# Loading, band, mixing and stores of a convolution plus spectral-mixing kernel: full-row loads, an on-chip band, four modes at a time, 8-tile stores

## The chip, the cores and the metric

The kernel runs on one core of one Trainium2 chip. Such a core has a matrix engine (TensorE, PE in the profile; its weight loads are listed as PEld), a vector engine (DVE), a scalar engine (ACT), GpSimd (POOL), and SyncE (SP), which here only issues DMAs. Each engine works through its own queue in order; DMAs are carried out by 16 DMA engines. The metric is the device time of one execution in microseconds (us).

## The reference

`x` is [8, 3264, 192] in float32 (batch B, sequence S, channels D). It passes first through a causal convolution of 7 taps whose softmaxed weights differ by head (8 heads of 24 channels), then through a spectral step over the sequence: the first 64 Fourier modes are multiplied by a complex 192x192 matrix for each mode, transformed back and added, and a ReLU of a channel product is added to that.

```python
# convolution: w = softmax(weight) per head, x padded with 6 zero rows at the front
out = np.einsum('hk,bskhg->bshg', w, x_unf)
# spectral step on u0 = out
X  = np.fft.rfft(x, axis=1);  Xr, Xi = real(X[:, :64]), imag(X[:, :64])
Yr = einsum('bmd,mde->bme', Xr, w_r) - einsum('bmd,mde->bme', Xi, w_i)
Yi = einsum('bmd,mde->bme', Xr, w_i) + einsum('bmd,mde->bme', Xi, w_r)
y  = np.fft.irfft(Y, n=S, axis=1)
u  = x + y
return u + np.maximum(u @ w_ch, 0.0)
```

## The kernel before

The sequence is cut into 27 windows of 122 rows; a window is loaded with the 6 rows ahead of it, so it fills 128 partitions. All of x stands in SBUF as bf16 (`x_all`), and the convolved values overwrite it in place. A batch is worked on in three units of 10, 8 and 9 windows.

1. **Load (POOL's DMA queue).** `load_mid` (L63) loads the windows of one unit, all 128 rows. Windows 0 and 26 of all eight batches come in two DMAs of their own (L71 with 122 partitions, L73 with 98), which are issued second and fourth. At most eight DMAs of this queue are outstanding; each issue waits for the one eight places before it.
2. **Band and Fourier tables (setup).** The softmax is worked out on 8 partitions, written to a DRAM scratch (`vdram`), read back as `hank` (L116) in a skewed form and reversed into `cband` (L118), a 128x128 band for each head. DVE prepares the angles, ACT the sines (`fst`, L143).
3. **Convolution stage.** For each batch: eight matmuls a unit against `cband` into two PSUM buffers (L208), ACT casts them back into `x_all` (L214); `dft` is 27 matmuls against `fst` into one PSUM buffer `xp` (L247), which DVE copies to `xs` (L250); `xtrans` transposes `xs` (L257, L259) and DVE spreads it into `xt` (L261). In between `t_part` transposes the convolved windows (L225: 128 channels at a time; L222: the last 64 channels of two windows, side by side on two column halves), and DVE copies them into `cT` (L241).
4. **Mixing stage.** It needs `xt` of all batches. For two modes at a time (a group `wt`, two DMAs of 144 KB, five buffers) the weights are the stationary operand and `xt` (16 columns) moves: 12 matmuls a group (L306). Every 8 modes DVE and ACT copy the result into `yeT` (L316, L318). The rest of the transposes is interleaved here.
5. **Output stage.** 54 groups, each of two windows of two batches: PE forms `zp` (inverse transform and channel product, L355 to L360) and `yp` (L361); ACT takes the ReLU (L366, three buffers `r`), DVE adds `x_all` (L374) into `t` (three buffers), POOL or, every third time, DVE adds `r` (L377), SP stores `t` with four DMAs (L385), of 112 and of 10 rows for each batch.

The order on each engine is set by the framework's scheduler, from the program's order and its dependencies; waits are semaphores.

Of the kernel before, what the change touches and what calls it, by code (L numbers as in the profile page):

```python
# [18 lines left out]
def kernel(  # L19
# [33 lines left out]
    dramp = ctx.enter_context(tc.tile_pool(name="dscr", bufs=1, space=bass.MemoryType.DRAM))  # L53
# [35 lines left out]
    xt = ep.tile([P, 3, MODES, 2 * B], BF16, tag="xt")  # L89

    vdram = dramp.tile([H, 256], BF16, name="vdram")
    with tc.tile_pool(name="setup", bufs=1) as sp:
        wrev = sp.tile([H, KK], F32, tag="wrev")
        nc.sync.dma_start(out=wrev[:], in_=bass.AP(tensor=weight.tensor, offset=weight.offset,
                                                   ap=[[KK, H], [1, KK]]))
        vrow = sp.tile([H, 256], BF16, tag="vrow")
        nc.vector.memset(vrow[:], 0.0)
        nmax = sp.tile([H, 1], F32, tag="nmax")
        nc.vector.reduce_max(out=nmax[:], in_=wrev[:], axis=AX.X)
        wsub = sp.tile([H, KK], F32, tag="wsub")  # L100
        nc.vector.tensor_scalar(out=wsub[:], in0=wrev[:], scalar1=nmax[:, 0:1], scalar2=None,
                                op0=ALU.subtract)
        wexp = sp.tile([H, KK], F32, tag="wexp")
        nc.scalar.activation(out=wexp[:], in_=wsub[:], func=ACT.Exp)
        wsum = sp.tile([H, 1], F32, tag="wsum")
        nc.vector.reduce_sum(out=wsum[:], in_=wexp[:], axis=AX.X)
        nc.vector.tensor_scalar(out=wsum[:], in0=wsum[:], scalar1=1e-9, scalar2=None, op0=ALU.add)
        wrec = sp.tile([H, 1], F32, tag="wrec")
        nc.vector.reciprocal(out=wrec[:], in_=wsum[:])

        nc.vector.tensor_scalar(out=vrow[:, 127:127 + KK], in0=wexp[:], scalar1=wrec[:, 0:1],
                                scalar2=None, op0=ALU.mult)
        nc.sync.dma_start(out=vdram[:], in_=vrow[:])
        va = vdram[:]
        hank = sp.tile([P, H, P], BF16, tag="hank")
        nc.sync.dma_start(out=hank[:], in_=bass.AP(tensor=va.tensor, offset=va.offset,  # L116
                                                   ap=[[1, P], [256, H], [1, P]]))
        nc.vector.tensor_copy(out=cband[:], in_=hank[:, :, ::-1])  # L118
# [6 lines left out]
                       allow_small_or_imprecise_dtypes=True)  # L125
        kprod = sp.tile([P, NWIN, MODES], F32, tag="kprod")
        nc.vector.tensor_tensor(out=kprod[:],
# [3 lines left out]
        for comp in range(2):  # L131
            targ = sp.tile([P, NWIN, MODES], F32, tag=f"targ{comp}")
            shift = float(S // 4) if comp == 0 else 0.0
            nc.vector.tensor_scalar(out=targ[:], in0=kprod[:], scalar1=shift, scalar2=1.0 / S,  # L134
                                    op0=ALU.add, op1=ALU.mult)
            nc.vector.tensor_scalar(out=targ[:], in0=targ[:], scalar1=MAGIC, scalar2=None, op0=ALU.add)
            nc.vector.tensor_scalar(out=targ[:], in0=targ[:], scalar1=-MAGIC, scalar2=-float(S),
                                    op0=ALU.add, op1=ALU.mult)
            nc.vector.scalar_tensor_tensor(out=targ[:], in0=targ[:], scalar=shift, in1=kprod[:],
                                           op0=ALU.add, op1=ALU.add)  # L140
            nc.vector.tensor_scalar(out=targ[:], in0=targ[:], scalar1=-float(S) / 2,
                                    scalar2=float(S) / 2, op0=ALU.max, op1=ALU.min)
            nc.scalar.activation(out=fst[:, :, MODES * comp:MODES * comp + MODES], in_=targ[:],  # L143
                                 func=ACT.Sin, scale=(TWOPI / S) * (1.0 if comp == 0 else -1.0))


    for b in range(1, B):
        load_mid(b, 1, 9)
        load_mid(b, 10, 8)
        load_mid(b, 18, 8)  # L150
# [28 lines left out]
    yeT = [constp.tile([P, B, 2 * MODES], BF16, tag=f"yeT{t}", name=f"yeT{t}") for t in range(2)]  # L179
    zwi = constp.tile([P, 2, B, D], BF16, tag="zwi")  # L180
# [6 lines left out]
    wp = early_stack.enter_context(tc.tile_pool(name="wts", bufs=5, side="right"))  # L187
# [7 lines left out]

    ps1 = ExitStack()
# [19 lines left out]
    def t_slot(o, b, slot):  # L216
        i, r = divmod(slot, 3)
        w = min(2 * i, NWIN - 2) if r == 2 or (i == PAIRS and r == 1) else 2 * i + r
        idw = ident[0:WIN, 0:WIN]
        if r == 2 or (i == PAIRS and r == 1):  # L220
            for k in range(2):
                nc.tensor.transpose(o[64 * k:64 * k + 64, :], x_all[0:WIN, b, w + k, P:D], idw,  # L222
                                    tile_position=(0, 64 * k))
        else:
            nc.tensor.transpose(o, x_all[0:WIN, b, w, 0:P], idw)  # L225
# [6 lines left out]
    def t_unit_halves(b, u):  # L232
        s0, n = USLOTS[u]
        h1 = (n + 1) // 2
        return [(b, s0, h1), (b, s0 + h1, n - h1)]

    def t_part(b, s0, n):
        tp = ptr.tile([P, 8 * WIN], BF16, tag="tp")
        for k in range(n):
            t_slot(tp[:, WIN * k:WIN * k + WIN], b, s0 + k)  # L240
        nc.vector.tensor_copy(out=cT[:, b, WIN * s0:WIN * (s0 + n)], in_=tp[:, 0:WIN * n])  # L241
# [11 lines left out]
    def xtrans(b, xs):  # L253
        tp = pxx.tile([P, 3, P], F32, tag="xt")
        xsv = xs[:, :].rearrange("k (p j) -> k j p", j=3)
        for j in range(3):
# [5 lines left out]
            out=xt[:, :, :, b:2 * B:B].rearrange("p j m c -> p j c m"),  # L262
# [3 lines left out]
    tq = []  # L266
    pend = None
    for b in range(B):
        for u in range(3):
            conv_unit(b, u)  # L270
            if u == 0 and b > 0:
                pend = (b - 1, dft(b - 1))
            if u == 1 and pend is not None:
                xtrans(*pend)
                pend = None
            if b < 5:
                for _ in range(2):
# [147 lines left out]
```

## Time and profile before

| | us |
|---|---|
| median of 3 runs (lowest, highest) | 309.76 (309.28, 312.28) |
| the profiled execution: its time | 309.76 |
| the profiled execution: its span | 308.0 |
| busy in the span: PE, DVE, POOL, ACT | 201.0, 142.8, 136.9, 99.8 |

The span is the time between the first and the last event that the profile shows; 1.76 us lie outside of it. No engine is busy for more than two thirds of the span, so the shares say little; the stages have to be read one by one. A matmul's end is modelled, so a busy PE is not PE at its peak. [...]

### The profile page before, as it was taken

The page shows a single profiled execution, that of the slowest core. Times are in us where ns is not written, and L with a number is a line of the kernel's source. Part 1 is how long each engine was busy: PE and PEld are TensorE (multiplying, and loading weights), DVE is VectorE, ACT ScalarE, POOL GpSimd, SP SyncE. Part 2 cuts the span into 40 slices and gives each one's busy share as a digit, 9 for nine tenths or more (in the row PEclk, how much of TensorE's full clock was granted, in tenths as well). Part 3 has the DMA queues.
Part 4 walks back from the last instruction along what each step waited for, and adds up shares of the span by engine and source line. Part 5 has one row for each costly group of instructions (what it writes and reads, how often), then busy time and mean ns, then how long its engine had stood idle before and what let it go on. Part 6 is the DMA issues. An engine that isn't in the chain of part 4 may idle for free.

```text
span 308.0 us, 5139 instructions
## 1 busy us (share of the span) xinstructions
PE 201.0 (65%) x1971; PEld 144.0 (47%) x1971; DVE 142.8 (46%) x174; ACT 99.8 (32%) x123; POOL 136.9 (44%) x145
## 2 busy tenths in 40 slices
PE   0004865999999989996232598776775666665610
PEld 0003543776778966554232376545553544544500
DVE  6009902386454444443000155565566456556560
ACT  1003696001468822001000145333433434334320
POOL 8804644625000046336763044546546444564650
PEclk9999997899999975555555589799799999999975
DMA  8899999997500049657999026656565556656653
GB/s 93 49 180 191 191 191 192 192 145 100 91 2 3 0 56 166 95 81 111 176 202 157 0 63 180 177 135 178 151 183 159 142 153 168 178 159 168 180 162 85
DMA packets 74160, 40.73 MB, mean 132 GB/s; under 512 B 39824, under 2 KB 74136, under 8 KB 74136
## 3 DMA queue, kind: packets, MB, share of 16 engines
q0 software_dynamic: 44240, 20.08, 50.5%
q1 hardware_dynamic: 29896, 20.33, 24.7%
q8 instruction: 15, 0.25, 0.3%
q14 instruction: 9, 0.07, 0.1%
HBM read 40.35 MB, written 20.06 MB: 196 GB/s over the span
## 4 chain that ended last, share of the span: by engine, by line
PE 35%; DMA 24%; POOL 12%; DVE 8%; ACT 7%; issue 6%; SPq 6%; DVEq 0%; POOLq 0%; ACTq 0%
DMA out_dram<-t 11%; POOL t L377 10%; PE tp L225 8%; DMA x_all<-in_x_dram 8%; PE tp L222 7%; PE xp L247 7%; DVE t L374 6%; SPq L385 6%; PE cp L208 5%; DMA wt<-in_moe_w_i_dram 5%; ACT x_all L214 4%; PE yps L306 2%; POOL wt L192 2%; ACT r L366 1%; PE tp L289 1%
## 5 line engine op out<-in xcount | busy, mean ns | idle before, releaser
L377 POOL TENSOR_TENSOR t<-t,r 122x768 f32<-122x768 f32 x36 | 64.8, 1806 | 70.0 <-DVE t L374 41.6
L374 DVE TENSOR_TENSOR t<-yp,x_all 122x768 f32<-122x768 f32 (+1 forms) x54 | 51.4, 956 | 49.7 <-DMA out_dram<-t 33.5
L366 ACT ACTIVATE r<-zp 122x768 f32<-122x768 f32 (+1 forms) x54 | 43.7, 810 | 70.8 <-POOL t L377 54.7
L214 ACT CAST x_all<-cp 122x960 bf16<-122x960 f32 (+2 forms) x48 | 39.0, 886 | 59.9 <-PE cp L208 59.8
L355 PE MATMUL zp<-zwi,gst 128*128 128x384 bf16 x108 | 36.7, 340 | 32.0 <-ACT r L366 28.6
L359 PE MATMUL zp<-win,cT 128*128 128x192 bf16 x216 | 48.7, 255 | 0.0
L208 PE MATMUL cp<-x_all,cband 128*128 128x240 bf16 (+2 forms) x192 | 26.7, 276 | 30.3 <-DMA x_all<-in_x_dram 26.7
L241 DVE COPY cT<-tp 128x854 bf16<-128x854 bf16 (+2 forms) x48 | 28.8, 606 | 38.1 <-PE tp L222 17.8
L192 POOL DMA_DIRECT2D wt<-in_moe_w_r_dram x32 | 19.3, 602 | 57.7 <-PE yps L306 47.3
L359 PEld LDWEIGHTS <-cT 128*128 128x128 bf16 x216 | 21.8, 101 | 42.7 <-issue 39.6
L64 POOL DMA_DIRECT2D x_all<-in_x_dram x24 | 25.2, 1057 | 27.5 <-DMA x_all<-in_x_dram 26.5
L225 PE MATMUL tp<-ident,x_all 122*128 122x122 bf16 x216 | 36.5, 255 | 0.0
L208 PEld LDWEIGHTS <-cband 128*128 128x128 bf16 x192 | 18.5, 104 | 35.2 <-DVE targ L134 26.7
L361 PE MATMUL yp<-zwi,gst 128*128 128x384 bf16 x108 | 28.9, 343 | 4.3 <-DVE t L374 4.3
L222 PE MATMUL tp<-ident,x_all 122*64 122x122 bf16 x224 | 31.6, 274 | 0.0
L306 PE MATMUL yps<-xt,wt 128*128 128x16 bf16 x384 | 14.9, 175 | 20.8 <-DMA wt<-in_moe_w_i_dram 14.6
L247 PE MATMUL xp<-x_all,fst 122*128 122x192 bf16 (+1 forms) x216 | 24.7, 260 | 3.9 <-ACT fst L143 3.9
L360 PEld LDWEIGHTS <-cT 128*128 128x128 bf16 x216 | 21.8, 101 | 9.9 <-issue 1.7
L360 PE MATMUL zp<-win,cT 128*128 128x192 bf16 x112 | 26.2, 257 | 0.0
L306 PEld LDWEIGHTS <-wt 128*128 128x128 bf16 x384 | 13.6, 105 | 22.6 <-issue 9.2
L360 PE MATMUL zp<-wB,cT 128*128 128x192 bf16 x104 | 22.5, 255 | 0.0
L192 POOL DMA_DIRECT2D wt<-in_moe_w_i_dram x32 | 19.6, 612 | 5.1 <-DMA x_all<-in_x_dram 2.9
(69 smaller groups left out, 185.6 us busy)
## 6 DMA issues: line engine op xcount, KB each, us to landing
out_dram<-t SPq DMA_DIRECT2D x104, 168.0 KB
x_all<-in_x_dram POOLq DMA_DIRECT2D x16, 384.0 KB, 16.7
wt<-in_moe_w_r_dram POOLq DMA_DIRECT2D x32, 144.0 KB, 4.8
wt<-in_moe_w_i_dram POOLq DMA_DIRECT2D x32, 144.0 KB, 5.1
x_all<-in_x_dram POOLq DMA_DIRECT2D x8, 432.0 KB, 16.9
out_dram<-t SPq DMA_DIRECT2D x104, 15.0 KB
out_dram<-t SPq DMA_DIRECT2D x2, 276.0 KB
x_all<-in_x_dram POOLq DMA_DIRECT2D x1, 366.0 KB, 23.3
```

The source lines that it names most:

```text
L192: nc.gpsimd.dma_start(out=wt[64 * half:64 * half + 64, :, :, :], in_=src[MG * g:MG * g + MG, :, :].rearrange("m (p j) e -> p m j e", j=3))
L208: nc.tensor.matmul(cp[:, j, 0:GRP * n].rearrange("p (w e) -> p w e", w=n), cband[:, h, :], x_all[:, b, w0:w0 + n, GRP * h:GRP * h + GRP], ...
L214: nc.scalar.copy(out=dst, in_=srcv)
L222: nc.tensor.transpose(o[64 * k:64 * k + 64, :], x_all[0:WIN, b, w + k, P:D], idw, tile_position=(0, 64 * k))
L225: nc.tensor.transpose(o, x_all[0:WIN, b, w, 0:P], idw)
L247: nc.tensor.matmul(xp[:, 0:D], fst[0:k, c, :], x_all[0:k, b, c, :], start=(c == 0), stop=(c == NWIN - 1))
L355: nc.tensor.matmul(zp[:, k, 0:2 * D], glhs, zwi[:, 0, 2 * q:2 * q + 2, :], start=True, stop=False)
L359: nc.tensor.matmul(o, cT[:, b, WIN * sa:WIN * sa + P], win0[:, 0:D], start=False, stop=False)
L360: nc.tensor.matmul(o, cT[:, b, WIN * sb:WIN * sb + P], wBs[par], start=False, stop=(i == 1))
L366: nc.scalar.activation(out=r[0:n, :, :], in_=zp[0:n, :, 0:2 * D], func=ACT.Relu)
L374: nc.vector.tensor_tensor(out=tv, in0=yv, in1=xv, op=ALU.add)
L377: eng.tensor_tensor(out=t[0:n, :, :], in0=t[0:n, :, :], in1=r[0:n, :, :], op=ALU.add)
```

## The change

- Loads go unit by unit in the order of use (`load_unit`), each of 128 partitions; windows 0 and 26 are now loaded with their unit. Only the first and the last window of all are loaded in two pieces (112 and 10 rows, 96 and 2 rows). For batches 1 to 7, window 0 is loaded with the 6 rows of the batch before, and DVE then overwrites those rows with zeros (L77).
- `cband` is built on the chip: the taps are broadcast to 128 partitions, POOL makes seven diagonal masks, and DVE adds them up with 56 instructions of 128x128. The angle tables take one chain of five DVE instructions, not two, and ACT makes the cosine from the absolute value.
- `dft` of a batch is written two batches later, not one; the transposes are nearly all left to the mixing stage. The last 64 channels of a unit are first copied together by DVE (`make_tail`), so that two windows are transposed by one matmul of 128 channels.
- Mixing: four modes at a time, each on its own 32 columns of the array. `xt` (of a mode and its neighbour, 32 columns) is now stationary and the weights (192 columns) move. ACT copies the product to `ymix`, two transposes bring it into the layout of before. Six `wt` buffers, not five.
- A `t` buffer holds two groups (8 tiles of 122x192), and is stored by four DMAs of twice the size. Still three buffers of `t` and of `r`.

```diff
+    def load_unit(b, u):
+        w0, n = UNITS[u]
+        if b == 0 and u == 0:
+            nc.gpsimd.dma_start(out=x_all[OV:OV + 112, 0, 0, :], in_=x[0, 0:112, :])
+            nc.gpsimd.dma_start(out=x_all[OV + 112:P, 0, 0, :], in_=x[0, 112:WIN, :])
+            load_win(0, 1, n - 1)
...
+        else:
+            load_win(b, w0, n)
+        if u == 0 and b > 0:
+            nc.vector.memset(x_all[0:OV, b, 0, :], 0.0)
...
-        nc.sync.dma_start(out=hank[:], in_=bass.AP(tensor=va.tensor, offset=va.offset,
-                                                   ap=[[1, P], [256, H], [1, P]]))
-        nc.vector.tensor_copy(out=cband[:], in_=hank[:, :, ::-1])
+        for h in range(H):
+            nc.vector.tensor_scalar(out=cband[:, h, :], in0=maskk[:, 0, :], scalar1=wsb[:, h, 0:1],
+                                    scalar2=None, op0=ALU.mult)
+            for k in range(1, KK):
+                nc.vector.scalar_tensor_tensor(out=cband[:, h, :], in0=maskk[:, k, :],
+                                               scalar=wsb[:, h, k:k + 1], in1=cband[:, h, :],
+                                               op0=ALU.mult, op1=ALU.add)
...
-    tq = []
+    tq = [(b, u) for b in range(B) for u in range(3)]
     pend = None
-    for b in range(B):
+    for b in range(B + 2):
         for u in range(3):
-            conv_unit(b, u)
-            if u == 0 and b > 0:
-                pend = (b - 1, dft(b - 1))
+            if b < B:
+                conv_unit(b, u)
+            if u == 0 and b >= 2:
+                pend = (b - 2, dft(b - 2))
...
-                for j in range(3):
-                    nc.tensor.matmul(o, wt[:, mj, j, 64 * t:64 * t + P], xt[:, j, m, :],
-                                     start=(j == 0), stop=(j == 2))
...
+    for g in range(MODES // 4):
+        yp = pconv.tile([P, 512], F32, tag="cv", name="yp")
+        for j in range(3):
+            for pos in range(4):
+                m = 4 * g + pos
+                wt = wtiles[m // MG]
+                nc.tensor.matmul(yp[32 * pos:32 * pos + 32, 0:D],
+                                 xt[:, j, m:m + 2, :].rearrange("p m k -> p (m k)"),
+                                 wt[:, m % MG, j, :], start=(j == 0), stop=(j == 2),
+                                 tile_position=(0, 32 * pos))
+        ymix = workp.tile([P, D], BF16, tag="ymix")
+        nc.scalar.copy(out=ymix[:], in_=yp[:, 0:D])
+        if tq:
+            t_unit(*tq.pop(0))
...
-            for i in range(2):
-                dst = out[2 * q0 + i, WIN * w0:WIN * (w0 + 2), :].rearrange("(k p) e -> p k e", k=2)
-                for r0, r1 in ((0, 112), (112, WIN)):
-                    nc.sync.dma_start(out=dst[r0:r1], in_=t[r0:r1, :, D * i:D * i + D])
...
+            t = p3.tile([P, 4, 2 * D], F32, tag="t")
+            npair = min(2, PAIRS - i0)
+            for i in range(i0, i0 + npair):
+                group([(q, 2 * i), (q, 2 * i + 1)], t, 2 * (i - i0))
+            store(q, 2 * i0, 2 * npair, t)
```

Two places show how the engines' queues change. The first is DVE's queue between the angle tables and the first copy of `xp` to `xs`. Before, the tables are followed by copies of transposes (`cT`) and then by `xs`:

```order
L139 SCALAR_TENSOR_TENSOR targ<-targ,kprod 128x1728 [waits DVE_49] x2
L141 TENSOR_SCALAR targ<-targ 128x1728 [waits DVE_49] x2
L183 MEMSET cT 128x8x3 [waits DMAHW1_49,Activation_49]
L241 COPY cT<-tp 128x976 [waits PE_49]
L241 COPY cT<-tp 128x854 [waits PE_49]
L241 COPY cT<-tp 128x732 [waits PE_49] x2
L250 CAST xs<-xp 128x192 [waits PE_49]
```

In the changed kernel the seven memsets of L77 stand among the tables and ahead of the first `xs` (L275); each waits on one of the eight semaphores of POOL's DMA queue (DMASW), that of its batch's first unit. Ahead of this piece stand those of batches 1 to 4; the three in it are those of batches 5, 6 and 7 (`tl` is the tail of a unit):

```order
L152 TENSOR_SCALAR kprod<-kprod 128x1728 [waits DVE_49]
L233 COPY tl<-x_all 122x640 [waits DMASW2_49,DMASW1_49,Activation_49]
L233 COPY tl<-x_all 122x512 [waits Activation_49]
L77 MEMSET x_all 6x96 [waits DMASW1_49]
L235 COPY tl<-x_all 122x512 [waits DVE_49,DMASW4_49,PE_49,Activation_49]
L236 COPY tl<-x_all 122x128
L77 MEMSET x_all 6x96 [waits DMASW4_49]
L194 MEMSET cT 128x8x3 [waits Activation_49]
L266 COPY cT<-tp 128x976
L266 COPY cT<-tp 128x854
L77 MEMSET x_all 6x96 [waits DMASW7_49]
L275 CAST xs<-xp 128x192 [waits PE_49]
```

So the first `xs` has moved behind the landing of the first unit of the last batch.

The second place is PE's queue where the first `xs` is transposed. In the changed kernel it comes right behind the 66th of the 192 convolution matmuls (before: behind the 80th, and nothing ahead of its `xs` on DVE waits for a load):

```order
L220 LDWEIGHTS cband [waits DMASW2_49]
L220 MATMUL cp<-x_all,cband 128x216 [waits Activation_49]
L220 LDWEIGHTS cband
L220 MATMUL cp<-x_all,cband 128x216
L282 LDWEIGHTS xs [waits DVE_49]
L282 MATMUL tp<-ident,xs 64x128
L284 LDWEIGHTS xs
L284 MATMUL tp<-perm,xs 64x128 [waits Pool_49]
```

Everything behind these rows on PE, 126 convolution matmuls among them, has moved behind that copy on DVE.

## Rows read from the trace of the kernel before

**Rows 1.** Windows by stage: us, busy time (instructions) by engine, PEclk, DMA share, GB/s.

```profile
0.00:26.70 26.70, 0.00 (x0) 0.00 (x0) 9.02 (x17) 1.49 (x2) 13.00 (x18) 1.00 1.13 118
...
50.00:110.50 60.50, 59.51 (x630) 45.74 (x631) 32.48 (x46) 25.21 (x31) 13.27 (x25) 0.94 0.63 80
110.50:140.00 29.50, 29.43 (x328) 17.44 (x327) 12.05 (x22) 3.85 (x5) 13.08 (x22) 0.52 0.76 111
140.00:172.00 32.00, 10.51 (x254) 8.82 (x251) 5.17 (x8) 4.27 (x6) 18.93 (x32) 0.50 0.94 149
172.00:300.50 128.50, 85.83 (x664) 61.71 (x663) 72.39 (x76) 45.86 (x58) 64.81 (x36) 0.93 0.56 152
```

**Rows 2.** Windows, two stretches of the loads.

```profile
8.00:16.00 8.00, 0.00 (x0) 0.00 (x0) 0.00 (x0) 0.00 (x0) 6.03 (x10) 1.00 0.85 50
...
22.00:64.00 42.00, 29.76 (x224) 20.12 (x225) 22.09 (x25) 20.75 (x23) 20.96 (x27) 0.92 1.60 192
```

**Rows 3.** Timeline of the opening: start, us, engine, line, operation [idle before].

```profile
3.31 3.51 POOL L71 DMA_DIRECT2D x_all<-in_x_dram  x1
...
26.75 1.76 PE L208 MATMUL cp<-x_all,cband 128*128 128x240 bf16 x8 [26.75 <-DMA x_all<-in_x_dram]
...
74.16 0.59 POOL L192 DMA_DIRECT2D wt<-in_moe_w_r_dram  x1 [1.45 <-DMA x_all<-in_x_dram]
```

**Rows 4.** Timeline of ACT late in the convolution stage, six casts a row.

```profile
93.56 4.80 ACT L214 CAST x_all<-cp 122x768 bf16<-122x768 f32 x6 [1.16 <-PE cp L208]
98.70 4.80 ACT L214 CAST x_all<-cp 122x768 bf16<-122x768 f32 x6 [0.34 <-PE cp L208]
```

**Rows 5.** Waits, the line of the weight loads: us in total, times, longest.

```profile
POOL wt L192 <- PE yps L306: 47.3, 11, 33.6
```

**Rows 6.** Timeline of PE early in the mixing stage: start, us, operation, count.

```profile
112.67 0.97 PE L289 MATMUL tp<-ident,fst 122*128 122x122 bf16 x8
...
113.86 0.31 PE L222 MATMUL tp<-ident,x_all 122*64 122x122 bf16 x2
```

**Rows 7.** Groups of instructions by form: busy us, mean ns | idle before.

```profile
L377 POOL TENSOR_TENSOR t<-t,r 122x768 f32<-122x768 f32 x36 | 64.8, 1806 | 70.0 <-DVE t L374 41.6 <-DMA out_dram<-t 21.9 <-ACT r L366 6.1
L374 DVE TENSOR_TENSOR t<-yp,x_all 122x768 f32<-122x768 f32 x52 | 49.5, 956 | 49.1 <-DMA out_dram<-t 32.9 <-PE yp L361 11.4 <-PE zp L360 2.8
...
L377 DVE TENSOR_TENSOR t<-t,r 122x768 f32<-122x768 f32 x16 | 17.3, 1081 | 1.6
...
L241 DVE COPY cT<-tp 128x854 bf16<-128x854 bf16 x24 | 14.6, 608 | 12.0 <-PE tp L222 7.2 <-PE tp L225 4.8
...
L139 DVE SCALAR_TENSOR_TENSOR targ<-targ,kprod 128x1728 f32<-128x1728 f32 x2 | 3.8, 1942 | 0.0
```

**Rows 8.** The chain that ended last, in the output stage: start, us, what.

```profile
240.71 0.16 PE zp L355
...
241.20 0.16 PE zp L355
...
242.29 0.97 DVE t L374
...
245.58 2.26 DMA out_dram<-t
247.88 0.96 DVE t L374
```

**Rows 9.** The same chain, around the ends of mixing and of the output stage.

```profile
110.57 0.75 PE yps L306 x24
...
171.06 0.72 ACT yeT L318
...
172.40 0.32 PE zwps L337
...
177.51 0.97 DVE t L374
...
299.42 1.04 DVE t L377
```

More of the change, by code (lines that the diff above doesn't have):

```diff
@@ L178 @@
     gst = constp.tile([P, GW], BF16, tag="gst")
-    yeT = [constp.tile([P, B, 2 * MODES], BF16, tag=f"yeT{t}", name=f"yeT{t}") for t in range(2)]
-    zwi = constp.tile([P, 2, B, D], BF16, tag="zwi")
+    yeT = constp.tile([P, 2, B, 2 * MODES], BF16, tag="yeT")
     stashp = ctx.enter_context(tc.tile_pool(name="stash", bufs=1))
@@ L194 @@
         wtiles.append(wt)
+    nc.vector.memset(xt[:, :, MODES, :], 0.0)
     ps1 = ExitStack()
@@ L214, in conv_unit, with make_tail, slot_lhsT @@
             nc.scalar.copy(out=dst, in_=srcv)
-    def t_slot(o, b, slot):
-        i, r = divmod(slot, 3)
[L218 to L223, printed above, removed]
-        else:
-            nc.tensor.transpose(o, x_all[0:WIN, b, w, 0:P], idw)
+    def make_tail(b, u):
+        w0, n = UNITS[u]
+        tl = workp.tile([P, 10, D - P], BF16, tag="tail")
+        if u < 2:
+            nc.vector.tensor_copy(out=tl[0:WIN, 0:n, :], in_=x_all[0:WIN, b, w0:w0 + n, P:D])
+        else:
+            nc.vector.tensor_copy(out=tl[0:WIN, 0:n - 1, :], in_=x_all[0:WIN, b, w0:w0 + n - 1, P:D])
+            nc.vector.tensor_copy(out=tl[0:WIN, n - 1:n + 1, :], in_=x_all[0:WIN, b, w0 + n - 2:w0 + n, P:D])
+        return tl
+    def slot_lhsT(b, u, tl, slot):
+        i, r = divmod(slot, 3)
+        w0 = UNITS[u][0]
+        if i == PAIRS:
+            if r == 0:
+                return x_all[0:WIN, b, NWIN - 1, 0:P]
+            j = NWIN - 1 - w0
+        elif r < 2:
+            return x_all[0:WIN, b, 2 * i + r, 0:P]
+        else:
+            j = 2 * i - w0
+        return tl[0:WIN, j:j + 2, :].rearrange("p w e -> p (w e)")
     def slot_of(w):
@@ new lines @@
+    for g in range(MODES // 4):
[12 more added lines that the diff above has]
+            t_unit(*tq.pop(0))
+        if gq:
+            g_part(gq.pop(0))
+        if g % 2 == 0:
+            et = pxx.tile([P, 2, 2, P], BF16, tag="xt", name="et")
+        for t in range(2):
+            nc.tensor.transpose(et[:, t, g % 2, :], ymix[:, 64 * t:64 * t + P], ident[:])
+        if g % 2 == 1:
+            m0 = 4 * (g - 1)
+            for t in range(2):
+                dst = yeT[:, t, :, :].rearrange("p b (c m) -> p b c m", c=2)[
+                    :, :, :, m0:m0 + 8].rearrange("p b c m -> p m c b")
+                srcv = et[:, t, :, :].rearrange("p g (q k) -> p (g q) k", q=4)[:, :, 0:16].rearrange(
+                    "p m (c b) -> p m c b", c=2)
@@ L335, in zwi_pair @@
             b = 2 * q + i
-            nc.tensor.matmul(zp[:, i, 0:2 * D], yeT[0][:, b, :], win0[:], start=True, stop=False)
-            nc.tensor.matmul(zp[:, i, 0:2 * D], yeT[1][:, b, :], win1[:], start=False, stop=True)
+            nc.tensor.matmul(zp[:, i, 0:2 * D], yeT[:, 0, b, :], win0[:], start=True, stop=False)
+            nc.tensor.matmul(zp[:, i, 0:2 * D], yeT[:, 1, b, :], win1[:], start=False, stop=True)
         for i in range(2):
@@ L347, with group @@
     npool = [0]
-    def group(combos):
+    def group(combos, t, k0):
         zp = pz.tile([P, 2, 512], F32, tag="z")
```

183 lines of the change are left out of this document (81 added, 102 removed).

## The prediction

> **What bounds the kernel now.** I read the windows by stage first [rows 1]. The reader is to see five stages with five limits. Until 26.7 us PE does nothing. From 50 to 110.5 PE is busy for 59.5 of 60.5 us and sets the pace. From 110.5 to 140 it is full again, but at a granted clock of 0.52. From 140 to 172 it has 10.5 us of work in 32, and the DMAs run at 149 GB/s: the weights are awaited. From 172 to 300.5 no engine is full (PE 86, DVE 72, POOL 65 of 128.5 us) and the DMAs are at a share of 0.56.
>
> The opening is explained by the loads. In their steady state they move 192 GB/s, but from 8 to 16 us only 50 [rows 2]. What was issued just before is the 122-partition load of the windows 0 (L71 at 3.31); the first convolution matmul waits for a load until 26.75, and a weight load at 74.16 still waits for a load of x [rows 3]. Convolution and `dft` together, once the data are there, need 5.14 us a batch: ACT's six casts begin at 93.56 and again at 98.70 [rows 4]. The weights stop for 33.6 us in one piece because five groups are loaded and PE has not begun to mix [rows 5].
>
> The output stage is a ring. The chain goes from DVE's add at 242.29 through POOL's add and the store, which lands at 247.84, to the DVE add at 247.88, which needed that `t` buffer [rows 8]; L374 idled 32.9 us behind stores [rows 7]. From 177.51 to 300.46 [rows 9] is 123 us for 54 groups: 2.28 us a group, 6.8 a turn of three buffers.
>
> **The change, part by part.** The sum is made against the profiled execution, whose time, 309.76, is also the median; its span is 308.0, so 1.76 us lie outside.
>
> *Loads.* A window is 128x192 values of bf16, 49 KB; 216 windows at 192 GB/s [rows 2] take 55 us. The badly spread loads are gone. I let the flow begin at 4 us and charge 2 us for a gap (POOL makes the identity and seven masks between the second unit's load and the third's) and 2 us for a landing (a store lands in 2.26 [rows 8]): x is complete at about 63, where before the queue was still held at 74.16 [rows 3]. The weights follow; 12 DMAs of 147 KB at 192 GB/s are 9 us, done by 73, before anybody needs them.
>
> *Band.* 56 DVE instructions of 128x128. The nearest row is the same operation on 1728 elements, 1.94 us [rows 7]. By its elements alone 128 of them are 0.144 us, 8 us for 56; with 0.15 of fixed cost each it is 16.5. I take 14, from about 9 us (POOL has to make the masks behind four DMA issues) to 23. The angle chain follows with some 8 us. All this is hidden under the next item, for any price up to 25 us.
>
> *The memsets of L77.* This is where I expect the loss. They stand in DVE's queue, which is in order, and each waits for a load. The last angle instruction (L152) stands behind the memset of batch 4, whose first unit is complete with window 118: 118 x 0.256 = 30 us, so about 38. Behind the one for batch 7 (199 windows, 51 us, so about 59) stands the first copy of `xp` to `xs`. PE, also in order, needs that `xs` behind 66 of its 192 convolution matmuls, and then stands still; so does ACT, which casts what PE makes. Before, nothing in these queues waited for more than the batch at hand. PE reaches that point at about 47 (tables at 38, two sines and an absolute value on ACT about 5 us, a `dft` of 4 us at the low clock). The pause is thus about 12 us, and from 59 on 126 matmuls, 5.25 batches, remain: 5.25 x 5.14 [rows 4] = 27 us. PE restarts cold, as at 50, and the mean clock of 0.94 over the 60.5 us behind that [rows 1] means 7 us at the low level; I charge 3. The last `dft` and a half and two rounds of `xs` and `xt` cost about one more period and a DVE round trip, 7 us. Mixing starts at 59 + 27 + 3 + 7 = **96 to 97**, not at 110.6 [rows 9].
>
> That it is still earlier is due to what left this stage: 266 of the 440 transposes stood ahead of the first mixing matmul on PE, now 27 of 328 do.
>
> *Mixing.* Three limits lie close together. DMA: 52 transfers of 147 KB are still to come, 7.67 MB: 40 us at 192 GB/s [rows 2], 51 at the 149 of the stage before [rows 1]. DVE: 43 copies of 0.61 us [rows 7] are 26; 21 tails lie between 0.1 us (0.144 us for 128 elements, [rows 7], is the nearest row for one input) and a copy's 0.61 each, I take 0.35, 7 us; eight `yeT` copies 6 (ACT's twin took 0.72 [rows 9]); with gaps 43. PE: about 301 transposes of 128 channels, the two-window tails now in one. At the low clock eight such took 0.97 us with the end of the last [rows 6], so at most 0.12 each, 36 us (the pair of half-width ones, 0.31 in the same rows, is gone). The 192 mixing matmuls move 192 columns each; at the low clock 384 columns take 0.32 us [rows 9], so 0.16 each: 31 us if they follow one another, 8 if four run side by side. I take 8, since the 32 columns of a mode are its own, and with the 51 other transposes 6: 50 us at the low clock, some 27 at the high one. Of 40, 43 and 50 at worst I take **47 us**, against 61 before (110.57 to 171.78 [rows 9]): the end is at **144**. `ymix` and its transposes lie on ACT, 4.3 us busy of 32 before [rows 1], and cost nothing unless the last pair is late (1 us, within the 47).
>
> What PE's clock does here decides little in my sum. From 110.5 to 140 it stood at 0.52 while PE was full of transposes and 16-column matmuls, and from 50 to 110.5 at 0.94 with transposes between `dft` and convolution [rows 1]. [...]
>
> *Output.* The way from the last `yeT` to the first DVE add stays at 5.7 us (171.78 to 177.51 [rows 9]). A ring now holds six groups. To the 6.8 us of a turn come, for a buffer whose both adds are POOL's, 1.81 for the second add [rows 7], and for all buffers about 1.4 for the doubled store (375 KB at 271 GB/s, the rate at which a share of 0.56 with 152 GB/s [rows 1] would reach 1), and up to 0.96 for the second DVE add: 9 to 10 us for six groups, 1.6 a group, 85 us. Close behind stand DVE, 54 x 0.956 + 18 x 1.08 + 2.5 = 74; the DMAs, 20 MB at 271 GB/s = 74; PE, two windows a group of 0.66 us (0.49 from `zp` to `zp` and 0.16 for `yp` [rows 8]) = 71; POOL 65. Four queues that are 75 to 85% full hold one another up; I take 1.7 a group, **92 us**, within 78 (DVE plus 5%) and 123 (nothing gained). SP issues half as many DMAs; it held none up that I can price.
>
> Sum: 144 + 5.7 + 92 = 242; from the last add to the end 7.5 (300.46 to 308.0), 249; outside the span 1.8: **251 us**.
>
> **The rivals.** *A: the pause does not bite*, because the waits of L77 are met earlier than I reckon, or the first `xs` is not needed so soon. Then loads and ACT set the pace: mixing starts at about 79, the rest as above: 233. Against it speaks that both queues are fixed; for it, that the landing times are my estimate.
>
> *B: the output stage gains nothing*, since DVE, PE and DMA hold one another up so that 2.28 us a group remain: 251 + 31 = 282. For it: DVE and POOL adds alternate in one order, and a late one stops both. Against: L374 waited for stores for 33 of its 49 idle us [rows 7].
>
> *C: the four matmuls of a row of modes do not overlap.* At the low clock 12 of them are then 1.9 us [rows 9], PE needs 73 us for the mixing, the end is 26 us later: 277. Against it: in the trace the half-width transposes run in pairs in 0.31 us for two [rows 6], about as long as one with its tail. [...] No run here shows 32-column tiles.
>
> [...]
>
> **How the numbers follow.** Forecast 0.78, A 0.09, B 0.06, C 0.05, D 0.02. The predicted time is the forecast's, 251. Its own bounds are the output stage's 78 to 110 and the mixing's 41 to 55: 231 to 275 when not all go one way. That leaves out B, C, D and some of the forecast's tails, and takes in A: 231 to 275. Within 1% is about what a measurement of this kernel cannot tell from no change. All cases but D are faster by more than that: faster 0.97, same 0.01, slower 0.02.
>
> **What would show it.** Right: DVE idle on a load until 55 to 62 ahead of the first `xs`, with PE and ACT idle from about 47; no stretch of 50 GB/s in the loads; the first mixing matmul at 92 to 101; weights at 150 to 195 GB/s through the mixing; stores at a share of 0.7 to 0.85. Wrong: the first `xs` before 45 (then A); a PE that is full from 97 to 170 at 0.50 (C); L401 still idle behind stores for over half of its time, or a span of over 115 us from the first to the last add (B). The weakest term is the 92 us: nothing in the trace of before shows the output stage with a longer ring.

## The result and the profile after

The changed kernel takes 263.28 us (median of 4 runs, 261.74 to 265.93) against 309.86 (309.28 to 312.28) for the kernel before: a ratio of 0.847, 95% interval 0.840 to 0.853. The prediction was 251.0 us within 231 to 275. The execution that was profiled is the longest of the four, 265.93 us with a span of 264.2 (as are those of experiments 2, 259.27, of 3 with three buffers, 288.68, and of 7 with the mixing of before, 264.09); its rows are read against its own time.

The stages first, as windows of the changed kernel (columns as in [rows 1]; PEclk is the granted clock of TensorE as a share of its full one):

```profile
8.00:16.00 8.00, 1.28 (x4) 0.41 (x4) 8.00 (x32) 0.96 (x1) 6.69 (x9) 1.00 1.48 173
12.00:60.00 48.00, 17.86 (x106) 12.77 (x106) 17.79 (x53) 19.56 (x20) 21.34 (x30) 0.74 1.60 192
...
30.20:40.00 9.80, 0.00 (x0) 0.00 (x0) 2.91 (x4) 1.21 (x1) 3.79 (x5) 0.58 1.60 192
51.00:60.80 9.80, 0.55 (x7) 0.38 (x8) 1.58 (x6) 0.00 (x0) 4.37 (x13) 0.56 1.60 191
61.00:97.50 36.50, 35.36 (x385) 31.69 (x383) 17.11 (x17) 27.91 (x34) 6.40 (x11) 0.93 0.37 54
97.50:136.00 38.50, 31.25 (x462) 23.00 (x463) 31.47 (x77) 8.18 (x18) 25.38 (x44) 0.96 1.03 155
136.00:150.50 14.50, 5.62 (x75) 2.44 (x74) 3.29 (x6) 3.56 (x8) 4.92 (x9) 0.67 0.78 122
156.20:257.00 100.80, 76.61 (x648) 57.34 (x646) 76.04 (x75) 44.31 (x57) 69.16 (x36) 0.97 0.71 194
```

The 50 GB/s of [rows 2] are gone: from 12 to 60 us the loads run at 192 without a break. In two stretches of almost 10 us PE has almost no work although the data flow. From 61 on it is full, at 0.93 of its clock. Mixing has two parts: to 136 PE and DVE are both busy for 31 of 38.5 us, then nobody is. In the output stage the DMAs moved 194 GB/s, where [rows 1] had 152.

What made the two pauses stands in the timeline of DVE, and in the waits from 20 to 66 us (us in total, times, longest us):

```profile
25.21 0.14 DVE L77 MEMSET x_all<- 6x96 uint32 x1 [1.81 <-DMA x_all<-in_x_dram]
32.16 0.14 DVE L77 MEMSET x_all<- 6x96 uint32 x1 [5.90 <-DMA x_all<-in_x_dram]
39.04 0.14 DVE L77 MEMSET x_all<- 6x96 uint32 x1 [4.93 <-DMA x_all<-in_x_dram]
39.11 0.98 DVE L152 TENSOR_SCALAR kprod<-kprod 128x1728 f32<-128x1728 f32 x1
40.02 0.50 DVE L233 COPY tl<-x_all 122x640 bf16<-122x640 bf16 x2
...
52.88 0.14 DVE L77 MEMSET x_all<- 6x96 uint32 x1 [6.39 <-DMA x_all<-in_x_dram]
...
59.85 0.14 DVE L77 MEMSET x_all<- 6x96 uint32 x1 [5.73 <-DMA x_all<-in_x_dram]
59.91 0.28 DVE L275 CAST xs<-xp 128x192 bf16<-128x192 f32 x1
```

```profile
DVE x_all L77 <- DMA x_all<-in_x_dram: 30.2, 6, 6.4
...
PE tp L264 <- DVE tl L233: 10.4, 1, 10.4
...
PE tp L282 <- DVE xs L275: 10.1, 1, 10.1
```

Each of the short zeroings but the first waits for a load, 30.2 us in all. PE's first pause ends with the tail copy at 40.02, which the transposes need; its second with the `xs` at 59.91.

The output stage by groups of instructions, 157 to 258 us:

```profile
L404 POOL TENSOR_TENSOR t<-t,r 122x768 f32<-122x768 f32 x36 | 69.2, 1944 | 43.2 <-DVE t L401 32.4 <-DMA out_dram<-t 7.9 <-ACT r L392 2.7
L401 DVE TENSOR_TENSOR t<-yp,x_all 122x768 f32<-122x768 f32 x52 | 48.1, 951 | 17.9 <-PE yp L388 14.6 <-DMA out_dram<-t 1.6 <-POOL t L404 1.1
...
L392 ACT ACTIVATE r<-zp 122x768 f32<-122x768 f32 x51 | 40.8, 809 | 45.5 <-POOL t L404 32.7 <-PE zp L387 9.1 <-PE yp L388 2.4
...
L404 DVE TENSOR_TENSOR t<-t,r 122x768 f32<-122x768 f32 x16 | 23.8, 1490 | 3.1 <-ACT r L392 2.6
```

Against [rows 7] two things moved. DVE's first add hardly waits for stores any more (1.6 us of 17.9 here, 32.9 of 49.1 before). And the second adds became longer: 1490 ns on DVE (1081 before), 1944 on POOL (1806 before), while the first add stayed at 951. By shortest, median and longest, the instructions of the second add's line:

```profile
L404 POOL TENSOR_TENSOR t<-t,r x36: 1797/1811/2545, 157.4 to 252.3; 122x768 f32<-122x768 f32 x36
...
L404 DVE TENSOR_TENSOR t<-t,r x18: 947/1358/2298, 161.6 to 256.0; 122x768 f32<-122x768 f32 x16, 92x768 f32<-92x768 f32 x2
```

And the chain of waits from 198 us on:

```profile
198.52 1.83 DVE t L401 x2
200.38 0.10 POOL t L404
200.56 2.49 POOL t L404
203.08 0.81 ACT r L392
203.94 0.32 PE zp L382
204.26 0.08 PE zp L386
```

POOL's add, which overlaps a second add of DVE begun at 200.25, takes 2.49 us in place of its shortest 1.80, and ACT's ReLU and PE's next group wait for it.

### The profile page after: what moved, and what is told of

It reads as the page before. It is cut to its first block, busy times and chain, and to the rows that moved or that the text cites. A ratio compares the mean times of both kernels' runs of the same rounds, so it can differ in the third digit from the quotient of the medians.

```text
span 264.2 us, 4507 instructions
## 1 busy us (share of the span) xinstructions
PE 172.3 (65%) x1699; PEld 130.4 (49%) x1699; DVE 154.7 (59%) x264; ACT 105.9 (40%) x140; POOL 138.7 (52%) x154
## 4 chain that ended last, share of the span: by engine, by line
PE 36%; DMA 27%; DVE 14%; POOL 12%; ACT 4%; issue 3%; SPq 1%; DVEq 0%; POOLq 0%; ACTq 0%
DMA x_all<-in_x_dram 18%; POOL t L404 7%; PE xp L272 7%; DVE t L401 6%; PE cp L220 5%; PE tp L264 5%; DMA wt<-in_moe_w_i_dram 5%; PE zp L382 4%; DMA out_dram<-t 4%; PE zp L386 4%; PE zp L387 4%; DVE cT L266 3%; PE yp L388 3%; ACT r L392 3%; PE yp L321 2%
## 5 line engine op out<-in xcount | busy, mean ns | idle before, releaser
L404 POOL TENSOR_TENSOR t<-t,r 122x768 f32<-122x768 f32 x36 | 69.2, 1944 | 43.2 <-DVE t L401 32.4
L386 PE MATMUL zp<-win,cT 128*128 128x192 bf16 x216 | 46.0, 250 | 0.0
L220 PE MATMUL cp<-x_all,cband 128*128 128x240 bf16 (+2 forms) x192 | 31.0, 297 | 20.4 <-DVE cband L128 16.4
L203 POOL DMA_DIRECT2D wt<-in_moe_w_r_dram x32 | 19.5, 611 | 44.2 <-PE yp L321 36.7
L386 PEld LDWEIGHTS <-cT 128*128 128x128 bf16 x216 | 21.4, 99 | 25.6 <-issue 23.8
L220 PEld LDWEIGHTS <-cband 128*128 128x128 bf16 x192 | 20.3, 111 | 26.3 <-DVE cband L128 17.6
L264 PE MATMUL tp<-ident,tl 122*128 122x122 bf16 x112 | 22.1, 228 | 11.1 <-DVE tl L233 10.9
L264 PE MATMUL tp<-ident,x_all 122*128 122x122 bf16 x216 | 26.4, 228 | 3.4 <-DVE cT L266 2.6
L404 DVE TENSOR_TENSOR t<-t,r 122x768 f32<-122x768 f32 (+1 forms) x18 | 25.7, 1430 | 3.3 <-ACT r L392 2.6
L388 PE MATMUL yp<-zwi,gst 128*128 128x384 bf16 x108 | 26.3, 331 | 1.2 <-DVE t L401 1.2
L387 PEld LDWEIGHTS <-cT 128*128 128x128 bf16 x216 | 21.4, 99 | 8.3 <-issue 0.7
L387 PE MATMUL zp<-win,cT 128*128 128x192 bf16 x112 | 24.0, 249 | 0.0
L264 PEld LDWEIGHTS <-x_all 122*128 122x128 bf16 x216 | 18.4, 103 | 7.2 <-issue 5.5
L272 PEld LDWEIGHTS <-fst 122*128 122x128 bf16 (+1 forms) x216 | 20.3, 106 | 2.3 <-ACT fst L156 1.2
## 6 DMA issues: line engine op xcount, KB each, us to landing
x_all<-in_x_dram POOLq DMA_DIRECT2D x9, 384.0 KB, 17.9
```

The lines of the kernel that those rows point to most:

```text
L220: nc.tensor.matmul(cp[:, j, 0:GRP * n].rearrange("p (w e) -> p w e", w=n), cband[:, h, :], x_all[:, b, w0:w0 + n, GRP * h:GRP * h + GRP], ...
L264: nc.tensor.transpose(tp[:, WIN * k:WIN * k + WIN], slot_lhsT(b, u, tl, a + k), ident[0:WIN, 0:WIN])
L272: nc.tensor.matmul(xp[:, 0:D], fst[0:k, c, :], x_all[0:k, b, c, :], start=(c == 0), stop=(c == NWIN - 1))
L386: nc.tensor.matmul(o, cT[:, b, WIN * sa:WIN * sa + P], win0[:, 0:D], start=False, stop=False)
L387: nc.tensor.matmul(o, cT[:, b, WIN * sb:WIN * sb + P], wBs[par], start=False, stop=(i == 1))
L388: nc.tensor.matmul(yp[:, k, 0:2 * D], glhs, zwi[:, 1, 2 * q:2 * q + 2, :], start=True, stop=True)
```

## The experiments

Each is an edit of the changed kernel. Stage times are from the profiled execution: first mixing matmul, end of the last `yeT`, first and last add of the output stage (97.57, 150.50, 156.22 and 256.98 us in the changed kernel). Experiment 1, in which the order on DVE came out as in the changed kernel, has 95.47, 146.56, 152.28 and 253.81 in an execution of 262.75 us; so 2 us between two profiles are no finding by themselves.

**1. The zeroings later in the program.**

```diff
-        if u == 0 and b > 0:                 # in load_unit
-            nc.vector.memset(x_all[0:OV, b, 0, :], 0.0)
             if b < B:
+                if u == 0 and b > 0:
+                    nc.vector.memset(x_all[0:OV, b, 0, :], 0.0)
                 conv_unit(b, u)
```

> Each zeroing of six rows of window 0 (L77) is moved in DVE's order from the place where the load is issued to the place where that batch's convolution is issued; nothing else changes. Theory (the zeroings hold the angle chain and the first xs behind loads, and PE and ACT behind these): first xs at 38 to 46 instead of 59.9, PE not idle for more than 5 us between 25 and 60, first mixing matmul at 72 to 80 instead of 97.6, time 238 to 246. Rival (loads of x, ACT's casts or the cold clock set the same pace once the wait is gone): first mixing matmul after 90, time 256 to 264.

263.03 us; first mixing matmul at 95.47. This did not test the theory, since DVE's order came out as before: the scheduler had put the zeroings back to where they were.

```profile
51.91 0.14 DVE L295 MEMSET x_all<- 6x96 uint32 x1 [6.40 <-DMA x_all<-in_x_dram]
...
58.86 0.14 DVE L295 MEMSET x_all<- 6x96 uint32 x1 [5.71 <-DMA x_all<-in_x_dram]
58.93 0.28 DVE L273 CAST xs<-xp 128x192 bf16<-128x192 f32 x1
```

**2. Window 0 loaded without the foreign rows**, so that no zeroing has to wait.

```diff
+        elif u == 0:
+            nc.gpsimd.dma_start(out=x_all[OV:OV + 112, b, 0, :], in_=x[b, 0:112, :])
+            nc.gpsimd.dma_start(out=x_all[OV + 112:P, b, 0, :], in_=x[b, 112:WIN, :])
+            load_win(b, 1, n - 1)
         else:
             load_win(b, w0, n)
-        if u == 0 and b > 0:
-            nc.vector.memset(x_all[0:OV, b, 0, :], 0.0)
-    nc.vector.memset(x_all[0:32, 0, 0, :], 0.0)
+    nc.vector.memset(x_all[0:32, :, 0, :], 0.0)
```

> Window 0 of every batch is loaded from row 6 on, in two DMAs of 112 and 10 rows, as batch 0 was, with the six rows zeroed once at the start: DVE has no zeroing that waits for a load. 14 more load DMAs. Theory (those waits made the two pauses of PE, 30 to 40 and 51 to 60 us): first xs at 38 to 46, first mixing matmul at 74 to 82 instead of 97.6, time 240 to 250. Rival 1 (the small loads of 10 rows slow the queue as the 122-row load did in the kernel before): loads of x end after 70 and the first mixing matmul is at 90 or later, time over 256. Rival 2 (mixing starts earlier but waits for weights that come no earlier): first mixing matmul at 74 to 82, last yeT still after 140, time 254 to 262.

254.79 us (254.18 to 259.27), 3% less. The first `dft` begins at 37.28 (44.85 in experiment 1) and the first `xs` comes at 41.82, as the theory had it, but the first mixing matmul only at 89.88: not the theory's 74 to 82, and not for rival 1's reason, since the loads did not slow (191 GB/s from 40 to 56 us). Another wait took the second pause over. The longest wait of PE, and two windows:

```profile
PE tp L286 <- POOL perm L170: 9.2, 1, 9.2
```

```profile
40.00:48.00 8.00, 7.77 (x72) 7.03 (x70) 0.71 (x2) 5.05 (x7) 4.02 (x5) 0.82 1.60 191
48.00:56.00 8.00, 0.00 (x0) 0.00 (x0) 0.00 (x0) 0.64 (x1) 4.29 (x6) 0.82 1.60 191
```

`perm`, the matrix of the second half of `xtrans`, is made by POOL behind all its issues of loads of x, and these wait for earlier loads to land (the last 16 in the changed kernel for 21.4 us together, each for 0.28 to 1.96). It is done at 56.93 here. In the changed kernel the last row of it is

```profile
51.65 0.25 POOL L168 TENSOR_SCALAR_AFFINE_SELECT perm<-perm 128x64 bf16<-128x64 bf16 x1
```

so there it was done at 51.90, 1.8 us after the second pause began (50.14), and hidden under the wait for `xs`. The other 5 us come with this experiment, which puts 14 more load DMAs ahead of `perm`.

**3. One group to a `t` buffer again; and six such buffers.**

```diff
-            t = p3.tile([P, 4, 2 * D], F32, tag="t")
             for i in range(i0, i0 + npair):
-                group([(q, 2 * i), (q, 2 * i + 1)], t, 2 * (i - i0))
-            store(q, 2 * i0, 2 * npair, t)
+                t = pt.tile([P, 2, 2 * D], F32, tag="t")   # pt: 3 buffers, or 6
+                group([(q, 2 * i), (q, 2 * i + 1)], t, 0)
+                store(q, 2 * i, 2, t)
```

> The stores alone are undone: a t buffer holds one group again, three buffers, four store DMAs per group. Theory (the ring of t set the output stage before, and six groups in it are what was gained): output back to about 2.28 us a group, 123 us in place of 101, time 282 to 288. Rival (the output stage is carried by the adds of DVE and POOL and by the ring of r, whatever the stores): time within 2% of 263.

> As the kernel with the stores undone (one group to a buffer, four store DMAs per group), but with six buffers: as many groups in the ring as in the changed kernel, in stores of half the size. Theory (the number of groups in the ring counts): time within 1% of 263. Rival (the larger stores count, by fewer issues on SP or fuller transfers): time 272 to 286.

285.48 us with three buffers: the output stage takes 125.5 us (154.25 to 279.74), and the wait of before is back:

```profile
L402 DVE TENSOR_TENSOR t<-yp,x_all 122x768 f32<-122x768 f32 x52 | 49.5, 956 | 49.0 <-DMA out_dram<-t 32.6 <-PE yp L389 10.3 <-PE zp L388 3.8
```

With six it is 264.33 us (261.63 to 264.81), and the stage 98.9 (152.60 to 251.50). So the number of groups in the ring brought the 22 us; the size of a store brought nothing that shows. DVE's second adds are the longest of all here, and the stage is none the longer for it:

```profile
L405 DVE TENSOR_TENSOR t<-t,r 122x768 f32<-122x768 f32 x16 | 30.0, 1876 | 2.0 <-ACT r L393 0.5
```

**4. Six buffers of `r`** (in bf16, so that they fit).

```diff
-        r = p3.tile([P, 2, 2 * D], F32, tag="r")
+        r = pr.tile([P, 2, 2 * D], BF16, tag="r")    # pr: 6 buffers
```

> r gets six buffers in place of three; to fit, it is kept in bf16 (the second add then reads bf16). Theory (the round of 10.4 us for six groups runs through r: a late add of POOL frees r late, ACT's next relu waits, and with it zp and PE): output 84 to 90 us instead of 101, ACT's idle time on POOL's add under 10 us of the 36, time 247 to 253. Rival (the order in which the adds alternate on DVE and POOL holds the round, r only shows it): output 97 to 101, time 259 to 264.

263.36 us, output 100.8 us: the theory falls. ACT still waits for POOL's add for 28.5 us. The second adds, which read `r` in bf16 now, are shorter than in the changed kernel (1944 ns on POOL, 1490 on DVE), and the stage is as long:

```profile
L405 POOL TENSOR_TENSOR t<-t,r 122x768 f32<-122x768 f32 x36 | 62.4, 1752 | 49.5 <-DVE t L402 39.5 <-DMA out_dram<-t 6.7 <-issue 3.0
...
L405 DVE TENSOR_TENSOR t<-t,r 122x768 f32<-122x768 f32 x16 | 21.1, 1319 | 0.8
```

**5. All second adds on DVE.**

```diff
-        eng = nc.gpsimd if npool[0] % 3 else nc.vector
+        eng = nc.vector
```

> All second adds are on DVE, POOL has none. Theory (DVE's and POOL's adds slow each other down when they run at once): the mean of a second add on DVE falls from 1.43 us to 1.0 to 1.1 with no instance of 1.7, DVE needs 54 x (0.95 + 1.05) = 108 us, output 110 to 116, time 272 to 278. Rival (the second adds on DVE are slow for a reason of their own, such as their operands): mean stays at 1.4, DVE needs 128 us, time 290 or more.

261.16 us, output 99.2 us. The line of the second adds, and the window of the stage:

```profile
L404 DVE TENSOR_TENSOR t<-t,r x54: 936/949/959, 154.1 to 251.3; 122x768 f32<-122x768 f32 x52, 92x768 f32<-92x768 f32 x2
```

```profile
153.00:252.30 99.30, 77.23 (x648) 57.46 (x646) 96.07 (x111) 45.14 (x57) 0.00 (x0) 0.98 0.72 196
```

Without POOL no such add on DVE takes over 0.96 us: the long ones are due to POOL. The theory is right in that, and wrong in its sizes: it had 1.0 to 1.1 us for an add, 110 to 116 for the stage and 272 to 278 for the time. DVE is full here, 96 of 99.3 us, and the stage is no longer than with POOL's help: 36 adds on POOL bought nothing.

**6. x added by PE**, in all groups (with the zeroings of 1, which change nothing, and the copies of 7), or in every second one, with no add on POOL.

```diff
-            nc.tensor.matmul(yp[:, k, 0:2 * D], glhs, zwi[:, 1, ...], start=True, stop=True)
+            nc.tensor.matmul(yp[:, k, 0:2 * D], glhs, zwi[:, 1, ...], start=True, stop=not viape)
+            if viape:                                 # all groups, or every second one
+                nc.tensor.matmul(yp[:, k, 0:2 * D], ident[0:nx, :], x_all[0:nx, 2*q:2*q+2, w, :],
+                                 start=False, stop=True)
...
+            nc.vector.tensor_tensor(out=tk, in0=yp[...], in1=r[...], op=ALU.add)   # the only add
```

> Late zeroings and shared copies together, and another output stage: PE adds x to yp by one more matmul of 384 columns per window (identity standing in the array, 108 in all), and DVE makes t in one add from yp and r; POOL and the second adds fall away. Theory (the two adds, their contention and POOL's length set the 1.87 us a group): PE then sets 1.6 to 1.75 us a group, output 86 to 95 us, time 222 to 232. Rival (stores and the PSUM buffers hold the stage at 1.87): output 100, time 234 to 240.

> Output stage alone: in every second group PE adds x to yp by one more matmul of 384 columns per window and DVE makes t in one add; in the others DVE makes both adds. POOL has none. DVE: 27 x 0.95 + 27 x 1.90 = 77 us; PE: 54 x 1.32 + 27 x 0.33 = 80 us; stores 74 to 80. Theory (with DVE alone making the adds DVE was full, with x on PE in all groups PE was; between them neither is): output 86 to 92 us in place of 101, time 249 to 255. Rival (the stores, at 0.75 of the DMAs, or the PSUM buffers hold the stage near 1.85 us a group): output 97 to 101, time 259 to 263.

In all groups: 258.4 us, output 93.9 us (154.54 to 248.45), with PE busy for all of 160 to 176 and 15.66 of the next 16 us. The forecast of 222 to 232 had counted on an earlier start of mixing, which edit 1 does not give; the stage itself came as the theory said. In every second group: 252.1 us (251.74 to 252.24), output 89.6 us:

```profile
160.00:190.00 30.00, 29.75 (x260) 22.75 (x259) 25.27 (x29) 16.78 (x21) 0.00 (x0) 1.00 0.83 228
153.20:242.90 89.70, 82.27 (x700) 62.08 (x698) 75.14 (x84) 44.72 (x57) 0.00 (x0) 0.99 0.79 218
```

Neither the stores nor the PSUM buffers hold the stage at 1.87 us a group; when POOL's adds go and DVE is relieved, PE is the next limit.

**7. Every second copy of `tp` to `cT` on ACT; and the mixing of before.**

```diff
+            if a == s0:
                 nc.vector.tensor_copy(out=cT[...], in_=tp[...])
+            else:
+                nc.scalar.copy(out=cT[...], in_=tp[...])
```

> Every second copy of tp to cT is ACT's. Theory (from 108 to 136 DVE's copies and tails set the pace of the mixing stage): DVE's busy time between the first mixing matmul and the last yeT falls by about 13 us, the stage takes 43 to 46 us instead of 53, the end being set by the weights at 175 to 190 GB/s, time 253 to 256. Rival (the weights, or PE's transposes, set the pace and DVE only runs along): 51 us or more, time 261 to 264.

```diff
-                nc.tensor.matmul(yp[32 * pos:32 * pos + 32, 0:D], xt[:, j, m:m + 2, :]..., wt[:, m % MG, j, :],
-                                 ..., tile_position=(0, 32 * pos))
+                nc.tensor.matmul(o, wt[:, mj, j, 64 * t:64 * t + P], xt[:, j, m, :],
+                                 start=(j == 0), stop=(j == 2))      # 384 in all, no ymix
```

> The mixing alone is undone: the weights stand in the array again, 384 matmuls of 16 columns with 384 weight loads, no ymix; the transposes and the rest stay. Theory (the column groups took work from PE that was on the path): the stage takes 60 to 66 us instead of 53, time 270 to 276. Rival (DVE's copies and the weights set the stage either way): 51 to 55 us, time within 1% of 263.

264.62 and 261.01 us: both theories fall, and the rivals hold to within 1 us. With the copies shared DVE was busy for 24.99 us of the mixing stage in place of 34.76 (31.47 and 3.29 in the windows above), and the stage took 53 us as before. With the weights standing in the array again it took 50.5 us (96.83 to 147.29), no longer than with the four column groups, though PE had 708 matmuls in it in place of 537, at a mean clock of 0.79:

```profile
96.80:147.30 50.50, 37.49 (x708) 33.48 (x707) 35.76 (x85) 7.15 (x10) 30.34 (x52) 0.79 1.00 154
```

**8. Mixing without most of the weight loads.** Only six groups are loaded.

```diff
-    for g in range(NGRP):
+    for g in range(6):
         wt = wp.tile([P, MG, 3, D], BF16, tag="wt")
...
-                wt = wtiles[m // MG]
+                wt = wtiles[(m // MG) % 6]
```

> Only the first six groups of weights are loaded and all 32 groups are mixed with these: 52 of 64 weight DMAs are left out, and so the output is not that of the reference. Theory, formed after sharing the copies and undoing the mixing moved nothing (the weights' DMAs, at a share of 0.9 and more and some 165 GB/s, set the mixing stage): the stage takes 40 to 45 us instead of 53, DVE over 90% busy in it, time 250 to 255. Rival (DVE's copies or PE's transposes set it): 50 us or more, time 260 to 264.

247.04 us. From the first mixing matmul to the last `yeT` it is now 33.9 us (95.76 to 129.63):

```profile
95.70:129.60 33.90, 29.04 (x500) 21.69 (x501) 29.48 (x73) 11.56 (x26) 0.00 (x0) 1.00 0.01 2
```

The stage is shorter than the theory's 40 to 45; to the first add, with the rest of the transposes behind the mixing, it is 41.6 us, where the changed kernel needs 58.7. So the arrival of the weights cost 17 us, with what hangs on it: the scheduler's order on PE is another one here, and the granted clock, 0.67 at the end of the stage in the changed kernel, is 1.00 throughout. Whether the rate at which the DMAs carry this layout (146 GB/s over the stage, 149 in [rows 1]) or the return of six buffers sets that arrival, no run tells apart. In the changed kernel POOL's weight loads waited for PE to give a buffer back for 11 us of the stage behind the first mixing matmul, and for a transfer for 2.2.

**9. Together**: the split loads, `perm` made ahead of the loads, shared copies, seven weight buffers, x on PE in every second group.

> Together: window 0 loaded from row 6 on; perm built ahead of the loads in POOL's order (after the split loads PE waited for perm, which POOL made behind all load issues, from 48 to 57 us); every second copy of tp to cT on ACT; seven weight buffers in place of six; x added on PE in every second group, no adds on POOL. Theory (the pauses were waits for the zeroings and then for perm; the weights' DMAs set the mixing; the adds set the output): first mixing matmul at 76 to 82, last yeT at 125 to 134, output 88 to 92, time 230 to 240. Rival (a third wait takes the place of perm's, or the weights come no earlier than in the kernel with split loads): first mixing matmul after 86 or last yeT after 138, time 242 to 246.

231.3 us (230.73 to 232.63), a ratio of 0.753 to the kernel before, interval 0.749 to 0.758. Convolution, mixing, output:

```profile
32.00:72.00 40.00, 35.34 (x361) 31.49 (x361) 13.58 (x14) 34.18 (x40) 24.45 (x40) 0.87 1.43 176
78.00:126.00 48.00, 34.94 (x536) 24.46 (x536) 24.69 (x58) 29.54 (x49) 29.38 (x50) 0.92 0.98 155
132.40:221.80 89.40, 81.86 (x699) 61.63 (x696) 75.06 (x84) 44.72 (x57) 0.00 (x0) 0.99 0.80 219
```

The first mixing matmul is at 78.04, 19.5 us earlier with both waits gone, in the theory's range. The mixing stage still takes 47.9 us (to 125.91), at 155 GB/s with seven buffers; the output takes 89.2 us. This version beats both kernels.

## Why the prediction was right, and where it was off

**Sum.** Against the median, 263.28, the forecast of 251 is 12.3 us short; against the profiled time, 265.93, 14.9: 1 in the start of mixing, 6 in the mixing, 9 in the output, and 1 less in the rest. No term came out shorter than forecast by more than 1 us, so nothing of note cancelled. The range is 44 us wide against a gain of 46.6, so that the time lies in it says little by itself.

**The pause: right, but there were two.** It was the wait of DVE on the zeroings of L77, with PE and ACT behind it; the first `xs` came at 59.91 (forecast 59), mixing at 97.57 (96 to 97). The forecast let PE stand still once, from 47 on; it stood still twice, since the tail copies are behind the same zeroings as the tables. That leaves the sum as it is, which starts from the first `xs`. Rival A put the kernel without the pause at 79; the combined version began at 78.04. What the text did not see is `perm`, which POOL makes behind its load issues: experiment 2, which takes the zeroings out of the way but delays `perm`, gained 8.5 us and not the 18 between 251 and A's 233.

**Loads and band: as priced.** 192 GB/s; the band's 56 instructions took 14.3 us (6.02 to 20.35, 14 forecast), 0.256 each, 0.11 over the 0.144 where the author had estimated 0.15; one batch of convolution takes ACT 5.14 us as in [rows 4]. Neither was undone in a run, so that the gain in the opening comes from the loads rather than from the band is argued, not shown.

**Mixing: mis-sized, 47 forecast, 52.9 measured.** The term was chosen between DMA's 40 and 51, DVE's 43 and PE's 50. The upper end of DMA's own bound, by the 149 GB/s of [rows 1], was the right one: experiment 7 shows that DVE's copies and the way of mixing moved nothing, experiment 8 that the weights were worth 17 us at the same work for PE and DVE. Since mixing as before takes as long in this kernel, the four column groups themselves brought no time that shows here; that the stage is 8 us shorter than before (61.2, from 110.57 to 171.78, [rows 9]) comes from something else in the change (fewer transposes, one more buffer), which was not taken apart.

**Rival C: false.** The first of them in the timeline of PE:

```profile
97.57 0.68 PE L321 MATMUL yp<-wt,xt 128*32 128x192 bf16 x24 [1.21 <-DVE xt L286]
```

24 took 0.68 us. One after another, at the 0.08 us that one of 192 columns takes in the chain above, they would take 1.9. So they overlapped. Nor did the 50 us at the low clock come, which the prediction had put beside the 27 at the high one: with 301 transposes and the mixing matmuls interleaved the clock was 0.96 from 97.5 to 136.

**Output: mis-sized, 92 forecast, 100.8 measured; B false.** The ring of `t` was the cause before: undoing the stores costs 22 us, almost half of the gain of 46.6. The step that failed is "Four queues that are 75 to 85% full hold one another up; I take 1.7", a size with no row behind it; 1.87 us a group were measured. It took DVE's 74 and POOL's 65 us as independent. They came to 76 and 69, since the two lengthen each other's adds (DVE's 1490 ns in the mean, 947 alone in experiment 5; POOL's 2545 at most, 1797 at the shortest), and a late add holds ACT and PE. But that this lengthening makes up the 9 us is not shown, and two runs speak against it: with shorter second adds (experiment 4) the stage took 100.8 us all the same, and with longer ones (experiment 3, six buffers) 98.9. What is shown is that the adds hold the stage: removing POOL's costs nothing, relieving DVE too gives 89.6. Which of the rounds through `t`, `r` and the PSUM buffers closes at 1.87 us a group is not settled; `r` alone (in bf16) is excluded. Two readings in that sum do not hold: the 271 GB/s take a DMA share of 1 for the ceiling, though [rows 2] show 1.60 with the loads (the 228 over 30 us of experiment 6 are the most that the rows shown here have for stores); and the upper bound of the output is 123 in one place and 110 in the range.

**D, slower than before by a clock that stays at its low level (0.50 from 140 to 172 in [rows 1]) from the pause on: false.** It stood at 0.93 from 61 to 97.5 and at 0.97 in the output stage.

## What to carry to other kernels

Look for what stands behind a short instruction that waits for a DMA: 0.14 us of zeroing held three engines for 20 us, and when it was gone a constant that another queue made behind its DMA issues, more of them by then, held one of the pauses again; moving a line in the program need not move it in the engine's order. Before giving an engine less work, take away the suspected supply once (load little, use it again): a stage in which PE and DVE were both 80% busy for 38 of 53 us was bound by neither. Adds shared between DVE and POOL were not free capacity here (100.8 us of output with 36 of them on POOL, 99.2 with none); price the pair together.

## What the hardware showed that I had not expected

The second adds, whose operands both lie in SBUF, lengthened here with DVE and POOL side by side: DVE's took 949 ns in the median with POOL idle (experiment 5) and 1358 beside it (the changed kernel), 2298 at most; POOL's took 1797 ns at the shortest and 2545 at most. DVE's first add, with one operand in PSUM, did not: 946 ns in the mean without POOL and 951 with it. POOL's longest is 0.75 us over its shortest, less than one DVE add, and DVE's 1.35 over its median alone, less than one of POOL. What the two contend for is not shown.

TensorE's granted clock fell to 0.50 early in the mixing of experiment 7, where 16 columns move, and stayed at 1.00 in the same stretch of experiment 1, where the weights move. That the moving operand decides this is not shown: the same 16-column matmuls ran at 1.00 a little later, and the changed kernel dipped too, with the weights moving. The lines are two of experiment 7, one of the changed kernel and one of experiment 1:

```profile
104.00:112.00 8.00, 7.21 (x106) 6.86 (x104) 6.18 (x15) 1.17 (x2) 5.09 (x9) 0.50 1.20 199
120.00:128.00 8.00, 6.67 (x124) 5.49 (x122) 7.48 (x20) 0.72 (x1) 5.59 (x10) 1.00 1.08 160
108.00:112.00 4.00, 3.92 (x49) 2.95 (x48) 3.41 (x9) 0.89 (x2) 2.70 (x6) 0.73 1.21 197
104.00:112.00 8.00, 6.99 (x102) 4.95 (x98) 7.35 (x19) 1.36 (x3) 5.76 (x11) 1.00 1.20 198
```

The low stretch cost nothing that shows in experiment 7: its mixing took 50.5 us, and 51.1 in experiment 1.
